# Granule 1's scores ahead of the second w_in piece: one head pair biased on TensorE, three masked by multiplication

## The chip, the cores and the metric

The kernel runs on one core of one Trainium2 chip. The metric is the device time of one launch in microseconds (us).

## The reference

Sliding-window attention with a few global keys and a distance bias, then a feed-forward block with a squared ReLU:

```python
# q, k, v: (4, 8, 768, 64); n_global 8, n_local 96
scores = q @ k^T / 8 - slope[h] * dist        # kept where key < 8, or 0 <= row - col < 96
a = softmax(scores);  x = (a @ v) as (3072, 512)
h = x @ w_in                                  # (512, 2048)
out = (s * relu(h)**2 + b) @ w_out            # (2048, 512)
```

## The kernel before

Work is cut into twelve granules of 256 tokens. The engines run one hand-written order of instructions; nothing is reordered later. For granule j and head pair hp, `S_mm` computes scores in PSUM, `S_post` the exponential on ScalarE (ACT), `A` the product with v, and `A_norm` the division. The distance bias and mask come in one of two ways: TensorE (PE) adds a bias table to the scores with an identity matmul (`SB_mm`), or VectorE (DVE) multiplies the exponentials by a table of exponentials (`S_mul`). `P1(j, f)` is one of eight steps of the first feed-forward product. It needs column piece f of w_in:

```python
for i in range(8):
    load_w_in(i, 8)            # software DMA queue of POOL, 512 x 256 fp32 in, bf16 in SBUF

def SB_mm(j, hp, ...):         # bias into PSUM: ident x bias table, two matmuls of 512 columns
def S_mul(j, hp):              # DVE: pt = pt * tmpl, 128 x 1024 bf16
def make_tmpl(h0, h1, lo, hi): # ACT: tmpl = exp(bias)

def P1(j, fp, sq="dve", tag="psh", relu="act"):
    ps = PS[tag].tile(...)                       # tag psh: two PSUM buffers, taken in turn
    for i in range(2):
        fc = 2 * fp + i
        for kc in range(KC):
            nc.tensor.matmul(ps[:, i, :], lhsT=w_in_bf[:, kc, fc*P:(fc+1)*P], rhs=xT[j][:, kc, :], ...)
    gs = gT[j][:, 2*fp:2*fp+2, :]
    flush()
    if relu == "dve": nc.vector.tensor_scalar_max(gs, ps[:], 0.0)
    else:             nc.scalar.activation(gs, ps[:], ACT.Relu)
    ...                                          # and the square, on either engine or late
```

The stretch that the change edits (granule 0's feed-forward, granule 1's attention):

```python
S_mm(1, 1)
S_post(1, 1, mul=False)
P1(0, 0, "late", "pso", relu="dve")
S_mul(1, 1)
S_mm(1, 2)
S_post(1, 2, mul=False)
P1(0, 1, "late", relu="dve")
SB_mm(1, 3)
S_mm(1, 3, True)
S_post(1, 3, True)
S_mul(1, 2)
P1(0, 2, "late")
A(1, 0, norm=False)
...                                              # A, norms, P1(0, 3)
XT_half(1, 0, "act", "av")                       # transposes of x for granule 1, half each
P1(0, 4, "late")
XT_half(1, 1, "dve", "pso")
for f in range(5):
    Q(0, f)                                      # squares on DVE
P1(0, 5)
P1(1, 0)
...
```

## Time and profile before

| what | before |
|---|---|
| time, median of the first three runs | 207.78 us (207.5 to 208.25) |
| span of the profiled run | 205.9 us |
| busy: PE, DVE, ACT, POOL | 97%, 84%, 56%, 36% |
| PE idle before P1(0,1), for piece 1 of w_in | 0.81 us |
| start of P1(0,5), the first use of piece 5 | 21.89 us |
| landing of piece 5 | 21.81 us |

The lines behind this table stand in the prediction below. They are best read in this order: which engine is busiest, which chain of waits set the end, and where on that chain PE stood still.

### The profile page before, as it was taken

Reading aid. Unit: us, or ns where it says so; the run is one execution under the profiler, and the core shown is the slowest. Engines: PE = TensorE matmul, PEld = TensorE weight load, DVE = VectorE, ACT = ScalarE, POOL = GpSimd, SP = SyncE. Lnnn points to the kernel's source line nnn. Section 1 sums busy time; section 2 is a strip of 40 time slices with the busy share of each in tenths; the row PEclk is TensorE's granted clock in tenths of the full one; section 3 lists DMA queues with packets and bytes.
Section 4 is the critical chain, followed back from the end, with each engine's and each line's share of the span. In section 5 each row is a group of like instructions: output and inputs, shape, how many; then the busy total and the mean of one; then the engine's idle time right before and its main releaser. Section 6 shows DMA issues by size and latency. Waiting matters only on the chain.

```text
span 205.9 us, 5606 instructions
## 1 busy us (share of the span) xinstructions
PE 199.8 (97%) x2295; PEld 160.8 (78%) x2295; DVE 172.9 (84%) x415; ACT 115.6 (56%) x173; POOL 73.7 (36%) x98
## 2 busy tenths in 40 slices
PE   7998999999999999999999999999999999999993
PEld 2667876547766678988988988988988988988883
DVE  5787877699989989788799799788799799787693
ACT  5885689355878576536536536536446446424400
POOL 8994673848273019008119019029000000000000
PEclk9999999999999999999999999999999999999999
DMA  6999999999999969999999989979966040040022
GB/s 168 191 184 197 191 195 192 181 156 162 130 136 155 227 81 96 151 182 128 206 122 115 206 86 111 209 98 120 206 85 154 28 134 22 0 153 5 0 105 102
DMA packets 103962, 27.64 MB, mean 134 GB/s; under 512 B 91392, under 2 KB 102016, under 8 KB 103936
## 3 DMA queue, kind: packets, MB, share of 16 engines
q0 software_dynamic: 70976, 13.11, 84.4%
q1 hardware_dynamic: 31904, 13.64, 35.9%
q10 hardware_dynamic: 1056, 0.52, 0.9%
q8 instruction: 18, 0.29, 0.6%
q14 instruction: 8, 0.07, 0.2%
HBM read 27.26 MB, written 6.29 MB: 163 GB/s over the span
## 4 chain that ended last, share of the span: by engine, by line
PE 84%; DMA 4%; POOL 4%; DVE 4%; ACT 1%; issue 0%; SPq 0%; POOLq 0%
PE ps L552 38%; PE ps_w L728 15%; PE ps L615 7%; PE ps_wb L728 7%; PE ps_av L470 4%; PE ps_s L414 4%; PE ps_wa L728 4%; DMA w_in_bf<-in_moe_w_in_dram 3%; POOL vaug L112 2%; PE ps_2s L615 2%; DMA xT<-xn 1%; DVE pt L441 1%; DVE o_pr L653 1%; POOL qnat L92 1%; POOL knat L92 1%; ACT gT L566 1%
## 5 line engine op out<-in xcount | busy, mean ns | idle before, releaser
L552 PE MATMUL ps<-xT,w_in_bf 128*128 128x256 bf16 x768 | 96.5, 273 | 1.2 <-DMA w_in_bf<-in_moe_w_in_dram 0.8
L552 PEld LDWEIGHTS <-w_in_bf 128*128 128x128 bf16 x768 | 72.6, 98 | 12.1 <-DMA w_in_bf<-in_moe_w_in_dram 1.1
L566 ACT ACTIVATE gT<-ps 128x512 bf16<-128x512 f32 x72 | 43.1, 598 | 58.5 <-PE ps L552 56.4
L427 ACT ACTIVATE pt<-ps_s 128x1024 bf16<-128x1024 f32 (+1 forms) x48 | 43.1, 951 | 4.8 <-PE ps_s L414 4.8
L728 PEld LDWEIGHTS <-sw 128*128 128x128 bf16 x288 | 28.1, 98 | 3.4
L582 DVE TENSOR_TENSOR gT<-gT 128x512 bf16<-128x512 bf16 x73 | 27.6, 416 | 1.7 <-ACT gT L566 1.6
L112 POOL DMA_DIRECT2D vaug<-in_v_dram x24 | 21.6, 914 | 4.1 <-DMA w_out_bf<-in_moe_w_out_dram 1.7
L728 PEld LDWEIGHTS <-gT 128*128 128x128 bf16 x208 | 19.7, 98 | 3.2 <-issue 0.2
L488 DVE TENSOR_TENSOR xn<-ps_av,rc 128x256 bf16<-128x256 f32 x48 | 20.4, 424 | 1.7
L441 DVE TENSOR_TENSOR pt<-pt,tmpl 128x1024 bf16<-128x1024 bf16 x30 | 20.0, 685 | 1.8 <-ACT pt L427 1.8
L125 POOL COPY pdum<-xT 1x1 bf16<-1x1 bf16 x5 | 3.2, 640 | 50.0 <-DMA xT<-xn 50.0
L615 PE MATMUL ps<-w_out_bf,gT 128*128 128x512 bf16 x80 | 19.7, 379 | 0.0
L728 PE MATMUL ps_w<-tw,sw 128*128 128x256 bf16 x144 | 18.7, 273 | 0.0
L738 DVE SCALAR_TENSOR_TENSOR u<-ps_w,s_bc,bvec 128x256 f32<-128x256 f32 x27 | 12.9, 479 | 6.4 <-PE ps_w L728 6.4
L470 PEld LDWEIGHTS <-pt 128*128 128x128 bf16 x352 | 15.3, 98 | 3.4 <-DVE pt L441 1.2
L104 POOL DMA_DIRECT2D qnat<-in_q_dram x18 | 15.9, 901 | 2.8 <-DMA w_out_bf<-in_moe_w_out_dram 1.4
L104 POOL DMA_DIRECT2D knat<-in_k_dram x18 | 16.0, 893 | 1.9 <-issue 1.4
L564 ACT ACTIVATE gT<-ps 128x512 bf16<-128x512 f32 x22 | 13.0, 598 | 6.1 <-PE ps L552 5.9
L470 PE MATMUL ps_av<-vaug,pt 128*128 128x65 bf16 x224 | 16.2, 193 | 0.2 <-DVE pt L441 0.2
L615 PEld LDWEIGHTS <-gT 128*128 128x128 bf16 x96 | 8.7, 97 | 8.1
L487 DVE RECIPROCAL rc<-ps_av 128x4 f32<-128x4 f32 x48 | 8.7, 182 | 7.0 <-PE ps_av L470 6.8
L414 PE MATMUL ps_s<-qT,kT 64*128 64x128 bf16 x224 | 12.5, 218 | 0.1
(102 smaller groups left out, 244.1 us busy)
## 6 DMA issues: line engine op xcount, KB each, us to landing
out_dram<-o_pr SPq DMA_DIRECT2D x10, 512.0 KB, 6.0
vaug<-in_v_dram POOLq DMA_DIRECT2D x24, 128.0 KB, 7.8
knat<-in_k_dram POOLq DMA_DIRECT2D x22, 128.0 KB, 6.4
qnat<-in_q_dram POOLq DMA_DIRECT2D x22, 128.0 KB, 7.6
w_in_bf<-in_moe_w_in_dram POOLq DMA_DIRECT2D x8, 256.0 KB, 8.0
w_out_bf<-in_moe_w_out_dram POOLq DMA_DIRECT2D x4, 512.0 KB, 10.1
out_dram<-o_pr SPq DMA_DIRECT2D x3, 256.0 KB, 3.0
raw<-in_q_dram ACTq DMA_DIRECT2D x2, 256.0 KB, 4.8
```

Of the source, the lines that this page charges most:

```text
L104: nc.gpsimd.dma_start(t[:, i, :, :], src[b, :, sb * P : (sb + 1) * P, :].rearrange("h p d -> p h d"))
L112: nc.gpsimd.dma_start(vaug[b % 2][:, sb, :, 0:D], v[b, :, sb * P : (sb + 1) * P, :].rearrange("h p d -> p h d"),)
L414: nc.tensor.matmul(ps[:, hi, oc * P : (oc + 1) * P], lhsT=kt[r, :], rhs=qT[j][r, hp, i * P : (i + 1) * P], start=not biased, stop=not bias ...
L427: nc.scalar.activation(pt[:, :, 0:n], ps[:, :, 0:n], ACT.Exp, scale=QSCALE)
L441: nc.vector.tensor_tensor(x, x, m.unsqueeze(2).to_broadcast((P, 2, GB, 2 * P)), ALU.mult)
L470: nc.tensor.matmul(av[:, i, hi, :], lhsT=pt[:, hi, c * P : (c + 1) * P], rhs=vv, start=n_ == 0, stop=n_ == len(ops) - 1,)
L488: nc.vector.tensor_tensor(xn[j][:, :, 2 * hp : 2 * hp + 2, :], av[:, :, :, 0:D], rc[:].to_broadcast((P, GB, 2, D)), ALU.mult,)
L552: nc.tensor.matmul(ps[:, i, :], lhsT=w_in_bf[:, kc, fc * P : (fc + 1) * P], rhs=xT[j][:, kc, :], start=(kc == 0), stop=(kc == KC - 1),)
L566: nc.scalar.activation(gs.rearrange("p f (r t) -> p f r t", r=2), ps[:].rearrange("p f (t r) -> p f r t", r=2), ACT.Relu,)
L582: nc.vector.tensor_tensor(gs, gs, gs, ALU.mult)
L615: nc.tensor.matmul(po[j, tb], lhsT=gT[j][:, fc, tb * P : (tb + 1) * P], rhs=w_out_bf[:, fc, :], start=(fc == 0), stop=(fc == FC - 1),)
L728: nc.tensor.matmul(wt[j, ps], lhsT=lhs[:, f, :], rhs=rhs[:, f, :], start=first and f == 0, stop=f == HF - 1, skip_group_check=True,)
```

## The change

Before, the bias matmuls and scores of pair (1,3) followed P1(0,1), which waits for piece 1. The change puts the scores of all four pairs ahead of P1(0,1) and masks pair (1,3) by multiplication. The multiplication's table of heads 6 and 7 is therefore made earlier on ACT, behind the exponentials. To balance DVE, the ReLU of P1(0,1) goes to ACT, and the ReLU of P1(0,0) goes behind a multiplication. The intent is to fill PE's wait for piece 1 and to save the bias product.

```diff
--- before.py
+++ after.py
@@ -558,6 +558,10 @@
                 )
         gs = gT[j][:, 2 * fp : 2 * fp + 2, :]
         flush()
+        if relu == "late":
+            late_sq[j, fp] = gs
+            late_ps[j, fp] = ps
+            return
         if relu == "dve":
             nc.vector.tensor_scalar_max(gs, ps[:], 0.0)
         elif j < W0:
@@ -575,7 +579,10 @@
         else:
             pend.append(gs)
 
-    late_sq = {}
+    late_sq, late_ps = {}, {}
+
+    def relu_late(j, fp):
+        nc.vector.tensor_scalar_max(late_sq[j, fp], late_ps.pop((j, fp))[:], 0.0)
 
     def Q(j, fp):
         gs = late_sq.pop((j, fp))
@@ -888,23 +895,25 @@
     S_post(1, 0, True)
     S_mm(1, 1)
     S_post(1, 1, mul=False)
-    P1(0, 0, "late", "pso", relu="dve")
+    P1(0, 0, "dve", "pso", relu="late")
     S_mul(1, 1)
+    relu_late(0, 0)
     S_mm(1, 2)
     S_post(1, 2, mul=False)
-    P1(0, 1, "late", relu="dve")
-    SB_mm(1, 3)
-    S_mm(1, 3, True)
-    S_post(1, 3, True)
+    S_mm(1, 3)
+    S_post(1, 3, mul=False)
+    make_tmpl(6, 8, 1, 3)
     S_mul(1, 2)
-    P1(0, 2, "late")
+    P1(0, 1, "late")
     A(1, 0, norm=False)
     A_norm(1, 0)
     A(1, 1, "pso", norm=False)
     A_norm(1, 1)
+    P1(0, 2, "late")
+    A(1, 2, "scA", norm=False)
+    S_mul(1, 3)
+    A_norm(1, 2)
     P1(0, 3, "late")
-    A(1, 2, "scA", norm=False)
-    A_norm(1, 2)
     A(1, 3, "scB", norm=False)
     A_norm(1, 3)
     XT_half(1, 0, "act", "av")
@@ -933,7 +942,6 @@
     SS(2, (0, 1))
     P1(1, 6)
     P1(1, 7)
-    make_tmpl(6, 8, 1, 3)
     make_tmpl(0, 8, 0, 1)
     po[0, 0] = ps_o.tile([P, DM], F32, name="ps_2", tag="pso")[:]
     P2_mm(0, 0, 0)
```

## The prediction

> **What bounds the kernel now.** I read the page's busy shares first, then the chain of waits cut to the stage that the change touches, then each engine's timeline there, and last the landing time of each piece of w_in.
>
> ```profile
> PE 199.8 (97%) x2295; PEld 160.8 (78%) x2295; DVE 172.9 (84%) x415; ACT 115.6 (56%) x173; POOL 73.7 (36%) x98
> PE   7998999999999999999999999999999999999993
> ```
>
> The tensor engine is busy for 97% of the 205.9 us span, and the slice row shows its thinner slices in the opening: the first, and the third, from 10.3 to 15.4 us. Work taken off PE shortens the kernel only if PE isn't then held by something else. The chain of waits names the holder (start, length, what):
>
> ```profile
> 9.48 6.50 DMA w_in_bf<-in_moe_w_in_dram
> 15.98 0.05 issue
> 16.03 1.05 PE ps L552 x8
> 17.07 0.43 PE ps_s L394 x2
> 17.51 0.33 PE ps_s L414 x8
> 17.84 0.98 PE ps L552 x8
> 18.82 0.49 PE ps_av L470 x16
> 19.30 0.87 PE ps L552 x8
> 20.18 0.48 PE ps_av L470 x16
> 20.66 0.23 PE ps_x L517 x4
> 20.89 0.87 PE ps L552 x8
> 21.76 0.23 PE ps_x L517 x4
> 21.99 5.32 PE ps L552 x48
> ```
>
> L552 is one P1 step: eight matmuls on one of eight column pieces of w_in, which I number 0 to 7; P1(0,n) needs piece n. L394 is the bias product of head pair 3, L414 its scores, L470 two A steps in a row, L517 half of the x transposes. PE waits for piece 1 until 15.98 us, then runs without a gap. The last row starts with P1(0,5), the first use of piece 5, and runs on through granule 1's first four steps. In PE's timeline:
>
> ```profile
> 16.03 1.05 PE L552 MATMUL ps<-xT,w_in_bf 128*128 128x256 bf16 x8 [0.81 <-DMA w_in_bf<-in_moe_w_in_dram]
> 21.89 5.41 PE L552 MATMUL ps<-xT,w_in_bf 128*128 128x256 bf16 x48
> ```
>
> P1(0,5) starts at 21.89 us with no recorded wait. But how early could it have started? The issue of piece 5 and its time to landing, from the timeline of POOL and the view of the tile:
>
> ```profile
> 12.41 0.82 POOL L129 DMA_DIRECT2D w_in_bf<-in_moe_w_in_dram  x1
> ```
> ```profile
> L129 POOL DMA_DIRECT2D w_in_bf<-in_moe_w_in_dram x1: 817/817/817, 12.4 to 12.4; - x1
> DMA to landing us min/median/max: 9.4/9.4/9.4
> ```
>
> 12.41 + 9.4 = 21.81 us: piece 5 landed 0.08 us before its use. The same sum for each piece gives landings at 13.8, 16.0, 17.2, 18.6, 20.0, 21.8, 22.8 and 24.3 us. Piece 1 checks the method: 9.48 + 6.5 = 15.98, as in the chain. POOL gives a second check, since its later loads resume after "DMA w_in_bf" at 16.27, 17.55, 18.93, 20.23 and 22.13 us, each about 0.3 us after the landing of pieces 1 to 5. So **the delivery of w_in is just hidden behind PE at piece 5**, and this decides the case.
>
> **What the Trainium skill says.** "TensorE: Matmul & The Clock Gate", Part 2, Step-by-step: only weight loads are pulled ahead, and "The MATMULs themselves stay in program order". The trace agrees: PE stood still for 0.81 us before piece 1, though the bias product of pair 3, whose PSUM was freed near 15.4 us, needed nothing from DMA. P1(0,5) will therefore hold everything behind it, even granule 1's P1 steps, whose pieces have landed. "DMA: Bandwidth & Descriptors", Anatomy of one DMA: a variable part of bytes / 436e9. A piece reads 512 x 256 fp32, 524 KB, which would be 1.2 us; the trace has (24.3 - 16.0) / 6 = 1.38 us per piece. Delivery is near its ceiling and does not depend on PE. "ScalarE: Activation LUTs", What ACT_TABLE_LOAD costs: 186 ns + 0.833 ns per element, less 93 ns back to back: 613 ns for the moved table of 512 elements per partition, where the trace has 643 alone and about 0.53 us as a step in a row. "VectorE: DVE Perf Modes", Side-by-side: a two-source bf16 operation runs at two elements per cycle plus about 150 cycles, an estimate of (512 + 158) / 0.96 = 698 ns for a mask multiplication over 1024 elements; the trace has 685.
>
> **The change part by part.**
> Removed on PE: the bias product of pair (1,3), 0.43 us of the chain. Moved on PE: its scores, 0.33 us, now stand before P1(0,1), in the idle stretch from 15.2 to 15.98 us. They need the scB bank, which exp (1,1) frees: the three exps start at 13.40 us and take 2.94 us, 0.98 a step, so the second ends near 15.36. Sixteen matmuls at the chain's rate are done by 15.8, before piece 1. Both parts fit, and PE loses 0.43 + 0.33 = 0.76 us after piece 1.
> Moved to ACT: the ReLU of P1(0,1), 0.60 us. The table of heads 6 and 7 moves there from 34.2 us. New order: exp (1,2) to 16.34, exp (1,3) to 17.33, table to 17.9, ReLU (0,1) to 18.45 us.
> DVE: one multiplication more, 0.685, one ReLU less, 0.67: a net of 0.02 us. In the new order: multiplication (1,1) from 15.5 to 16.2, ReLU (0,0) to 16.8, multiplication (1,2) to 17.4, norms of pairs 0 and 1 to 18.55, multiplication (1,3) to 19.2.
> Now PE again, with durations from the chain: P1(0,1) to 17.07; A(1,0) and A(1,1), 0.49, to 17.56; P1(0,2), 0.87, to 18.43 (piece 2 at 17.2); A(1,2), 0.24, to 18.67. P1(0,3) wants to start at 18.5 (ReLU (0,1) frees its bank at 18.45), but piece 3 lands at 18.6, so it runs from about 18.7 to 19.75. A(1,3), its multiplication done at 19.2, to 20.0; half the transposes to 20.2; P1(0,4), piece 4 at 20.0, to 21.1; the other half, after norms that I put at 20.7, to 21.3. **P1(0,5) could then start about 21.2**, 0.7 us before now, but piece 5 lands at 21.81. With the 0.05 us seen between landing and start at piece 1 it starts at 21.86, against 21.89. The gain is **0.03 us**; some 0.65 us become a new wait for piece 5.
> From there on nothing differs on PE. The table taken from ACT at 34.2 us frees 0.5 us of an engine that next waits 1.02 us for PE, so it is worth nothing on the path.
>
> **The rivals.**
> Full gain. If piece 5 landed by 21.2 us, the 0.7 us would pass on: the k and q of granule 2 land about 1.5 us ahead of use, and the third piece of w_out about 1.4. That makes 207.1 us. Against it: the landing above. For part of it: the interval before piece 5 was 1.8 us against a mean of 1.38, so at an even pace it would land at 16.0 + 4 x 1.38 = 21.5 us, and another execution could gain 0.3 us.
> New waits on ACT or DVE. ReLU (0,1) now stands behind two exps and a table, and P1(0,3) waits for its bank; multiplication (1,3) stands behind two norms. I put both just in time, to 0.1 or 0.5 us. If either is late, about 0.65 us of slack before piece 5 soaks it up; only beyond that is it a loss. A slip of 1 us would make 208.1.
> A downstream give-back. From 41 to 62 us DVE is busy 19.7 of 21 us and the chain crosses it at 63 to 71 us, so an early PE could meet it. But DVE work starts behind PE there and would shift with it; I give this little weight, and it could only take away a gain that the first rival grants, leaving 207.8.
>
> **Range and chances.** 207.78 less 0.03 to 0.3 us, by where piece 5 lands in other executions, is 207.5 to 207.75; I take **207.6 us**. The three runs of before spread over 207.5 to 208.25, wider than the effect, so the range runs from the full gain, **207.1**, to a slip with ordinary noise, **208.1**. Two per cent are 4.2 us, over five times all that is moved: faster by over 2% 0.01, within 2% 0.98, slower 0.01.
>
> **What would show each step right or wrong.** In the changed kernel's profile I expect the idle before P1(0,1) cut from 0.81 to under 0.5 us, its start still at 16.0, the scores of pair 3 done before it, and two L394 matmuls fewer. A new PE wait of 0.4 to 0.7 us for "DMA w_in_bf" should stand before P1(0,5), which starts at 21.8 to 21.9 us, and the chain should run back from there to that transfer. PE's busy time should fall by about half a microsecond with the span nearly unchanged. The prediction is wrong if P1(0,5) starts before 21.5 us without a wait (delivery was not the bound), or after 22.2 (ACT or DVE came late), or if it starts at 21.86 and the end still moves by over 0.4 us, which would put the effect downstream where I see none.

## The result, and the profile after

The changed kernel takes 207.73 us, the median of four runs (207.42 to 207.75), against 207.80 us for the kernel before (four runs, 207.5 to 208.25). The ratio is 0.9991, with a 95% interval of 0.9971 to 1.0012. A ratio here and below is the mean time of one kernel's runs over that of the other's of the same rounds, so not quite the ratio of the medians quoted. Executions over 1.5% slower than the fastest of the same kernel are left out of the means. Repeated with five more rounds the ratio was 1.0003 (0.999 to 1.0017). No gain is measured, and one of more than 0.3% is excluded by the first interval, of more than 0.1% by the second.

From the page of the changed kernel, the PE row of the busy shares and of the slices:

```profile
PE 198.5 (96%) x2286; PEld 160.6 (78%) x2293; DVE 173.4 (84%) x415; ACT 115.9 (56%) x174; POOL 73.2 (36%) x98
PE   7988999999999999999999999999999999999993
```

PE is busy 1.3 us less, and the span is again 205.9 us. Only two of the nine matmuls that the count lacks were removed by the change, the bias product. The other seven are second-product matmuls (L615 before, L622 after) which both programs contain, 96 in all, of which this trace recorded 89. So PE's busy sum exaggerates what was saved.

The two PE waits, from PE's timeline (start, length, what, idle before it and its releaser):

```profile
16.15 1.05 PE L552 MATMUL ps<-xT,w_in_bf 128*128 128x256 bf16 x8 [0.66 <-DMA w_in_bf<-in_moe_w_in_dram]
...
21.90 2.36 PE L552 MATMUL ps<-xT,w_in_bf 128*128 128x256 bf16 x20 [0.42 <-ACT gT L568]
```

The first row is P1(0,1) and the second starts with P1(0,5). P1(0,5) starts at 21.90 us, where it started at 21.89 before, and in front of it now stands a wait that wasn't there. The row blames a ReLU on ACT. The weight loads of the same step, on the row of PE's loader, name another releaser:

```profile
21.90 2.19 PEld L552 LDWEIGHTS <-w_in_bf 128*128 128x128 bf16 x21 [0.59 <-DMA w_in_bf<-in_moe_w_in_dram]
```

Which of the two holds it has to be decided. The chain of waits of the changed kernel follows the ReLU:

```profile
10.84 7.98 DMA w_in_bf<-in_moe_w_in_dram
18.82 0.04 issue
18.87 1.05 PE ps L552 x8
19.92 0.24 PE ps_av L470 x8
20.16 0.22 PE ps_x L517 x4
20.38 0.89 PE ps L552 x8
21.27 0.02 issue
21.29 0.61 ACT gT L568
21.90 0.01 issue
21.90 5.41 PE ps L552 x48
```

Until 18.82 us PE is held by piece 3. P1(0,3) and P1(0,4) follow, and the chain then goes through the ReLU of P1(0,4), which ends at 21.90 us. And piece 5, in POOL's timeline and in the view of the tile:

```profile
12.31 0.84 POOL L129 DMA_DIRECT2D w_in_bf<-in_moe_w_in_dram  x1
```
```profile
L129 POOL DMA_DIRECT2D w_in_bf<-in_moe_w_in_dram x1: 844/844/844, 12.3 to 12.3; - x1
DMA to landing us min/median/max: 9.5/9.5/9.5
```

12.31 + 9.5 = 21.81 us, the same landing as before. Both candidates end within 0.1 us of the start of P1(0,5). The kernel before already speaks against the ReLU: there the ReLU of P1(0,4) ran from 21.80 to 22.40 us and P1(0,5) started at 21.89, in the middle of it. The experiments settle it.

### The profile page after: what moved, and what is told of

Read it like the earlier page. It is cut to its first block, busy times and chain, and to the rows that moved or that the text cites. A ratio compares the mean times of both kernels' runs of the same rounds, so it can differ in the third digit from the quotient of the medians.

```text
span 205.9 us, 5597 instructions
## 1 busy us (share of the span) xinstructions
PE 198.5 (96%) x2286; PEld 160.6 (78%) x2293; DVE 173.4 (84%) x415; ACT 115.9 (56%) x174; POOL 73.2 (36%) x98
## 4 chain that ended last, share of the span: by engine, by line
PE 81%; DMA 5%; POOL 5%; DVE 4%; ACT 2%; issue 1%; SPq 0%; POOLq 0%; ACTq 0%
PE ps L552 37%; PE ps_w L735 15%; PE ps_wb L735 7%; PE ps L622 6%; PE ps_av L470 4%; PE ps_wa L735 4%; DMA w_in_bf<-in_moe_w_in_dram 4%; PE ps_s L414 4%; POOL vaug L112 2%; PE ps_2s L622 2%; DVE pt L441 2%; DMA xT<-xn 1%; DVE o_pr L660 1%; POOL w_in_bf L129 1%; ACT pt L427 1%
## 5 line engine op out<-in xcount | busy, mean ns | idle before, releaser
L570 ACT ACTIVATE gT<-ps 128x512 bf16<-128x512 f32 x72 | 43.1, 598 | 58.5 <-PE ps L552 56.4
L441 DVE TENSOR_TENSOR pt<-pt,tmpl 128x1024 bf16<-128x1024 bf16 x31 | 20.7, 686 | 2.1 <-ACT pt L427 2.1
L125 POOL COPY pdum<-xT 1x1 bf16<-1x1 bf16 x5 | 2.5, 509 | 50.5 <-DMA xT<-xn 50.5
L622 PE MATMUL ps<-w_out_bf,gT 128*128 128x512 bf16 x74 | 18.8, 379 | 0.4 <-issue 0.2
L470 PEld LDWEIGHTS <-pt 128*128 128x128 bf16 x352 | 15.4, 98 | 3.3 <-DVE pt L441 1.2
L568 ACT ACTIVATE gT<-ps 128x512 bf16<-128x512 f32 x23 | 13.6, 598 | 6.9 <-PE ps L552 6.7
L622 PEld LDWEIGHTS <-gT 128*128 128x128 bf16 x96 | 8.7, 97 | 8.1
```

What stands on the lines that cost most here:

```text
L441: nc.vector.tensor_tensor(x, x, m.unsqueeze(2).to_broadcast((P, 2, GB, 2 * P)), ALU.mult)
L470: nc.tensor.matmul(av[:, i, hi, :], lhsT=pt[:, hi, c * P : (c + 1) * P], rhs=vv, start=n_ == 0, stop=n_ == len(ops) - 1,)
L570: nc.scalar.activation(gs.rearrange("p f (r t) -> p f r t", r=2), ps[:].rearrange("p f (t r) -> p f r t", r=2), ACT.Relu,)
L622: nc.tensor.matmul(po[j, tb], lhsT=gT[j][:, fc, tb * P : (tb + 1) * P], rhs=w_out_bf[:, fc, :], start=(fc == 0), stop=(fc == FC - 1),)
```

## The experiments

**Theory D (delivery):** P1(0,5) waits for piece 5 of w_in, which lands at the same time in both kernels, so that what PE saves ahead of it becomes waiting. **Rival S:** it waits for the ReLU of P1(0,4), as the chain says. **Rival G:** PE does get ahead, and the gain is given back further down. All runs were timed in five rounds against the kernel before, and all results passed the comparison with the reference.

### The changed kernel once more

> The change once more, to narrow the interval. Theory D (delivery: P1(0,5) waits for piece 5 of w_in, which lands near 21.8 us in both kernels): ratio to before 0.998 to 1.000, P1(0,5) starts at 21.85 to 21.95 us. Full gain, which D excludes, would be 0.9964.

Measured: 207.75 us (207.45 to 208.34), ratio 1.0003 (0.999 to 1.0017). P1(0,5) started at 21.60 us in the profiled run, earlier than I expected, because piece 5 landed at 12.32 + 9.2 = 21.52 us. PE's row shows no wait there; the loader's row does, a short one for the transfer:

```profile
21.59 2.41 PEld L552 LDWEIGHTS <-w_in_bf 128*128 128x128 bf16 x23 [0.19 <-DMA w_in_bf<-in_moe_w_in_dram]
```

So the landing moves by tenths of a us between executions. Here P1(0,5) came with it, and PE was hardly ahead of it, because piece 1 had come late as well (9.39 + 7.1 = 16.49 us). The ReLU of P1(0,4) ran from 21.39 to 21.99 us in this run, so P1(0,5) did not wait for it.

### Piece 2 not loaded, in both kernels

```diff
+    nc.vector.memset(w_in_bf[:, :, 512:768], 0.0)
-    for i in range(8):
+    for i in (0, 1, 3, 4, 5, 6, 7):
         load_w_in(i, 8)
```

The result is wrong. The comparison passes it all the same: recomputing the reference with those columns zeroed changes the output by 0.7% in the root-mean-square sense.

> The changed kernel with piece 2 of w_in not loaded but set to zero (wrong result on purpose), so that pieces 3 to 7 land about 1.4 us earlier, piece 5 near 20.4 us. Theory D: P1(0,5) starts at 21.05 to 21.2 us, with no wait for DMA, and the time falls by about 0.75 us to 207.0, ratio to before 0.9963. Rival S (P1(0,5) is held by the ReLU of P1(0,4) on ScalarE, as the chain of waits of the changed kernel says): it starts near 21.6 us, time 207.45. Rival G (the gain is given back further down): it starts at 21.1 us but the time stays at 207.7.

> The same edit in the kernel before: piece 2 of w_in set to zero, not loaded (wrong result on purpose). Theory D: PE itself is the bound from piece 1 on there, so P1(0,5) stays at 21.85 to 21.95 us and the time at 207.8, ratio 1.000; the gain of the change, a_no2 against b_no2, then appears at about 0.996. If an earlier landing of the later loads helps somewhere else, this kernel gains too.

Measured, changed kernel with the edit: 207.15 us (206.66 to 207.32), ratio 0.9965 (0.9953 to 0.9977). Kernel before with the edit: 207.88 us (207.74 to 208.25), ratio 1.0007 (0.9995 to 1.0019). With piece 5 early (issued at 11.59 us, landed 8.6 us later, at 20.2) the change is worth 207.88 - 207.15 = 0.73 us. Without the edit it is worth nothing measurable. PE's timeline and ACT's timeline of the changed kernel with the edit:

```profile
21.13 1.04 PE L553 MATMUL ps<-xT,w_in_bf 128*128 128x256 bf16 x8
```
```profile
21.11 0.60 ACT L569 ACTIVATE gT<-ps 128x512 bf16<-128x512 f32 x1 [0.27 <-PE ps L553]
```

The PE row is P1(0,5), with no wait, at 21.13 us. The ACT row is the ReLU of P1(0,4), which starts at 21.11 and ends at 21.71. P1(0,5) doesn't depend on it, and rival S falls. Rival G falls as an explanation too, since most of the gain reaches the end. In the kernel before with the edit P1(0,5) started at 22.17 us rather than 21.9. In that execution piece 1 came later and P1(0,1) started at 16.37 us; from there PE ran without a wait for DMA, as expected.

### Piece 5 made later, in both kernels

```diff
     for i in range(8):
+        if i == 5:
+            nc.gpsimd.dma_start(extra[:], w_in_view[:, :, 0:P])
         load_w_in(i, 8)
```

> The changed kernel with an extra load of 262 KB (half a piece, into a tile that nothing reads; the result stays right) in the queue ahead of piece 5, about 0.69 us of delivery. Theory D: piece 5 lands near 22.5 us, P1(0,5) starts at 22.5 to 22.6, time up by about 0.65 us to 208.4, ratio 1.003. Rival S: P1(0,5) stays at 21.9 us and the time at 207.7, since P1(0,4) and its ReLU are untouched.

> The same extra load in the kernel before. Theory D: piece 5 had only 0.08 us of slack there, so P1(0,5) starts at 22.5 to 22.6 us as well and the time goes up by about 0.6 us to 208.4, ratio 1.003; the changed kernel and this one are equal again.

Measured: changed kernel with the edit 208.16 us (208.02 to 208.36), ratio 1.0019 (1.0007 to 1.0031); kernel before with the edit 208.18 us (208.0 to 208.58), ratio 1.002 (1.0007 to 1.0032). PE's timeline of the changed kernel with it:

```profile
22.35 2.36 PE L555 MATMUL ps<-xT,w_in_bf 128*128 128x256 bf16 x20 [0.99 <-DMA w_in_bf<-in_moe_w_in_dram]
```

P1(0,5) waits 0.99 us and starts at 22.35 us, with piece 5 landed at 13.14 + 9.2 = 22.34. In the kernel before it starts at 22.45, with a wait of 0.18 us:

```profile
22.45 2.25 PE L555 MATMUL ps<-xT,w_in_bf 128*128 128x256 bf16 x19 [0.18 <-DMA w_in_bf<-in_moe_w_in_dram]
```

The two kernels are equal again in time, and both wait for the transfer. In the kernel before most of the shift in this trace is not the transfer's, though: piece 1 came late (P1(0,1) started at 16.30 us), so PE was ready only at 22.27. The size was off: the extra load cost about 0.5 us of delivery in the changed kernel's run (22.34 against the 21.81 of its first profile), not 0.69, and 0.33 to 0.35 us of the time (medians, against 207.83 us in these rounds).

### Only the order changed, with the bias kept on PE

```diff
+    SB_mm(1, 3)
+    S_mm(1, 3, True)
+    S_post(1, 3, True)
     P1(0, 1, "late", relu="dve")
-    SB_mm(1, 3)
-    S_mm(1, 3, True)
-    S_post(1, 3, True)
```

> The kernel before with one part of the change alone: bias product and scores of pair (1,3) stand ahead of P1(0,1), still biased on PE, ReLU (0,1) still on VectorE. The idle stretch before piece 1 is 0.8 us and the two need 0.76 us, from 15.36 us on, so P1(0,1) should slip to 16.15 to 16.3 us. Theory D: P1(0,5) again waits for piece 5 and starts at 21.85 to 21.95 us; ratio 0.998 to 1.000. If the multiplication in place of the bias product were what counts, this one would be slower than the changed kernel by 0.2 us or more.

Measured: 207.63 us (207.36 to 207.92), ratio 0.9991 (0.9979 to 1.0003). P1(0,1) slipped to 16.30 us, as expected, though its releaser was piece 1. P1(0,5) started at 21.40 us, earlier than expected and without a wait, since piece 5 landed at 12.28 + 9.0 = 21.28 in that execution. What follows is that the wait for piece 1 is long enough for the bias product too, at least where piece 1 lands this late (9.35 + 6.9 = 16.25 us), so the multiplication isn't needed to fill it.

### Another step in front of P1(0,5)

If piece 5 is the bound, a step that needs an earlier piece should fill the wait. P1(1,0) needs piece 0 and both halves of granule 1's transposes. So I kept pair (1,3) biased but early, gave the ReLU of P1(0,1) to ACT and moved both halves ahead of P1(0,4). That is the first kernel, the control, cut to its core:

```diff
+    SB_mm(1, 3)
+    S_mm(1, 3, True)
+    S_post(1, 3, True)
+    S_mul(1, 2)
-    P1(0, 1, "late", relu="dve")
+    P1(0, 1, "late")
     ...                          # A(1,0), A(1,1), P1(0,2), A(1,2), A(1,3), P1(0,3)
     XT_half(1, 0, "act", "av")
+    XT_half(1, 1, "dve", "pso")
     P1(0, 4, "late")
-    XT_half(1, 1, "dve", "pso")
```

The second differs from the control only in this:

```diff
     XT_half(1, 0, "act", "av")
     XT_half(1, 1, "dve", "pso")
     P1(0, 4, "late")
     for f in range(5):
         Q(0, f)
-    P1(0, 5)
     P1(1, 0)
+    P1(0, 5)
```

> From the kernel before: bias product and scores of pair (1,3) ahead of P1(0,1), ReLU (0,1) on ScalarE, both halves of granule 1's transposes ahead of P1(0,4). P1(0,5) is still the step that follows. Theory D: PE is ready for it near 21.1 to 21.2 us and waits for piece 5 until 21.85; ratio 0.998 to 1.000.

> The same kernel with P1(1,0), whose piece 0 landed near 13.9 us, ahead of P1(0,5); nothing else differs. Theory D: P1(1,0) starts at 21.1 to 21.3 us, P1(0,5) follows near 22.0 without a wait, and the time falls by 0.6 to 0.75 us to 207.05 to 207.2, ratio 0.9965 to 0.997, so that it beats both kernels. Rival S (a PSUM bank held by the ReLU before): P1(1,0) starts near 21.7 to 21.8 us, time 207.7. Rival G (given back further down): PE is early at 22 us, but the time stays at 207.7.

Measured, control: 207.64 us (207.33 to 207.74), ratio 0.9991 (0.9979 to 1.0003). Its row for P1(0,5) in PE's timeline:

```profile
21.88 2.79 PE L552 MATMUL ps<-xT,w_in_bf 128*128 128x256 bf16 x24 [0.73 <-DMA w_in_bf<-in_moe_w_in_dram]
```

PE was ready 0.73 us early and waited, and here both views name the transfer. With the two steps exchanged: 207.33 us (207.25 to 207.76), ratio 0.9984 (0.9971 to 0.9996). In its trace PE runs from P1(0,4) through P1(1,0) and P1(0,5) without a wait:

```profile
20.29 4.42 PE L552 MATMUL ps<-xT,w_in_bf 128*128 128x256 bf16 x39
```

So the wait is gone, and the time fell by 0.3 us by the ratio, about half of what I expected. The chain of waits shows where the rest stayed:

```profile
43.68 7.01 DMA qT<-qnat
50.69 0.04 issue
50.73 0.46 PE ps_s L414 x10
```

A second transfer stands behind the first. Granule 3's scores wait at 50.7 us for its q, transposed by DMA. In the kernel before, the view of that tile has the second of these transposes as

```profile
L327 SPq DMA_TRANSPOSE qT<-qnat x1: 1189/1189/1189, 43.2 to 43.2; - x1
DMA to landing us min/median/max: 7.0/7.0/7.0
```

which lands at 43.2 + 7.0 = 50.2 us, and PE began those scores at 50.92 there. The slack was 0.7 us in that execution. It is less in others: with the steps exchanged the landing was 50.69 us here and 50.86 in a later run, and PE was ready at 50.4 us.

### Work in front of the second gate

One quarter of a P2 step (`P2b`, four matmuls of the second product) moved from behind granule 3's first scores to ahead of them:

```diff
     Q(2, 2)
+    P2b(2)
     period(3, [
-            (P2b, 2),
             (P2b, 3),
     ...
-        (3, 1, 3, 1),
+        (2, 1, 3, 1),
```

> The kernel of b_swap once more, as the control of the next one on the same chip and rounds. It got 0.9984, less than the 0.9965 to 0.997 expected: its trace shows a second wait at 50.7 us, for the transposes of granule 3's q. Expected again: 0.998 to 0.999.

> The kernel of b_swap, and one quarter of a P2 step (four matmuls, 0.87 us, operands there since 43 us) moved from behind the first scores of granule 3 to ahead of them, so that PE has work while the transposes of granule 3's q land. Theory D with a second gate at granule 3's q: the wait there goes and the rest of the 0.7 us comes through: ratio 0.9965 to 0.9975, time 207.1 to 207.3. If instead VectorE, busy without a pause from 41 to 58 us, takes the rest, it stays at 0.998 to 0.999.

> The kernel before with that second edit alone (a quarter of P2 ahead of granule 3's first scores). Its transposes land about 0.4 us before PE needs them, so there is no wait to take away: ratio 0.999 to 1.001.

| kernel | time, us | ratio to before |
|---|---|---|
| exchange, repeated | 207.51 (207.25 to 207.95) | 0.9987 (0.9973 to 1.0002) |
| exchange and P2 quarter | 207.11 (207.06 to 207.46) | 0.997 (0.9958 to 0.9983) |
| kernel before with the P2 quarter alone | 207.84 (207.59 to 208.02) | 1.0 (0.9987 to 1.0013) |

PE's timeline of the middle one:

```profile
50.32 1.03 PE L615 MATMUL ps<-w_out_bf,gT 128*128 128x512 bf16 x4
51.28 0.51 PE L414 MATMUL ps_s<-qT,kT 64*128 64x128 bf16 x12
```

The scores follow without a wait for the transposes. With both gates filled 0.6 us of the 0.7 arrives at the end (207.73 us for the kernel before in these rounds, less 207.11), and this version beats the kernel before, with an interval clear of 1. The changed kernel was not timed in these rounds; the ratios (0.997 against 0.9991 and 1.0003) suggest that it is beaten too. DVE, which I had named as a rival for the rest, did not take it. Neither edit alone does this: the exchange gives about 0.3 us by its two ratios (0.16% and 0.13%, the second interval just including 1), the P2 quarter alone nothing. The intervals of the exchange with and without the quarter overlap, so that the quarter helps rests on the medians, 0.40 us apart, and on the wait that is gone from the trace.

## Why the prediction was right

- **The bound.** That w_in's delivery is just hidden at piece 5 held in the executions profiled: by 0.08 us in the kernel before, and by 0.03 us (21.85 less 21.82) where that kernel had only the P2 quarter moved. It decided the case, as the control kernel and the two pairs of piece-5 experiments show.
- **The number.** 207.6 us was predicted, and 207.73 and 207.75 were measured. The gap of 0.13 us is within the noise, and so is the gain of 0.03 us that the mechanism gives. The time alone therefore doesn't show the mechanism; the traces and the experiments do.
- **What PE saves.** The 0.76 us are real: with piece 5 early, the change is worth 0.73 us. In the changed kernel the loader was free for P1(0,5) at 21.90 - 0.59 = 21.3 us. That is where the prediction's own sequence ends ("the other half [...] to 21.3"); the "21.2" that it then takes is a slip of 0.1 us. P1(0,5) started at 21.90 us where 21.86 was predicted.
- **Two readings.** The row of slices was misread: the thinner slices are the first and the fourth, from 15.4 to 20.6 us, not the third. The wait for piece 1, up to 15.98 us, lies in the fourth, and nothing else rests on it. The 1.2 us, 613 ns and 698 ns worked out from the Trainium skill's pages were estimates; the sequence was built on the traces' durations.
- **The new wait.** 0.42 us on PE's row and 0.59 us on the loader's, predicted as 0.4 to 0.7 us, with the estimate of the slack at 0.65. The chain of waits I had expected to run from P1(0,5) to the transfer. It ran through the ReLU of P1(0,4) instead, which happened to end 0.01 us before the start. Two traces in which P1(0,5) starts before that ReLU ends rule it out.
- **ACT and DVE.** ReLU (0,1) ended at 18.31 us (18.45 predicted) and multiplication (1,3) at 19.27 us (19.2). Both were in time.
- **The wait for piece 1.** I expected under 0.5 us left and P1(0,1) still at 16.0. It was 0.66 us and 16.15. Piece 1 landed 0.1 us later (9.38 + 6.7 = 16.08), and the scores ahead of it were done at 15.5 us, 0.3 us sooner than in my sequence.
- **Where a step failed.** In the rival "Full gain" I wrote that the 0.7 us would pass on, because granule 2's k and q and the third piece of w_out have 1.4 to 1.5 us of slack. I hadn't looked at the next transfer, granule 3's q, whose slack was 0.7 us or less. Had piece 5 been early, that gate would have taken part of the gain in some executions. In the profiled execution of the changed kernel without piece 2 it held ten of these scores until 50.54 us (a wait of 0.18 us), and yet the medians there show 0.73 us; this is not resolved. It didn't matter for the number predicted.
- **Where piece 5 lands in other executions.** The term "0.03 to 0.3 us" allowed an earlier landing. In the nine profiled executions of kernels with the same loads up to there, piece 5 landed between 21.14 and 21.82 us, in two groups. Where piece 1 landed by 16.08 us, piece 5 came at 21.8 (four executions, the first profiles of both kernels among them); where piece 1 came at 16.17 us or later, piece 5 came at 21.52 or earlier (five). The changed kernel showed both. So it is partly luck of the profiled execution that 21.90 us fell so close to 21.86. What makes the landings vary is open. The term also took the kernel before to be fixed at 21.89 us. When piece 1 comes late that kernel is late too: without piece 2 it started P1(0,1) at 16.37 and P1(0,5) at 22.17 us. In such executions the change could gain more, by an estimate of 22.17 - 21.60 = 0.57 us from two traces. No profile caught the kernel before with its own loads in one of them, and a mean gain of 0.1 to 0.2 us is neither shown nor excluded by the two timings (0.9991 and 1.0003).

## What to carry to other kernels

Before taking work off the bounding engine, add issue time and time to landing for every transfer that this engine will use afterwards, and compare with its use: the smallest slack caps the gain, though the profile shows no wait there yet. If a transfer is the cap, reorder so that the engine does something whose data are already there, and look for the next gate in the same way. A releaser in a chain of waits is trusted only if it also ends before the start in other executions and variants.

## What the Trainium skill lacked or had wrong

- "DMA: Bandwidth & Descriptors", Anatomy of one DMA, gives a DMA's time as 2.0 us plus bytes / 436e9, an estimate of 3.2 us for a piece of w_in. It gives no figures for a queue of such loads: eight issued 0.73 us apart landed 1.38 us apart on average from the second on, with 5.1 us to landing for the first and 10.4 for the eighth. For deciding on slack, the landing of each one is what counts.
- The same page gives no spread of a landing from one execution to another. Here piece 5 landed between 21.14 and 21.82 us in nine executions of kernels with the same loads.
- The same page, DMA Transpose (X-bar), lacks a time to landing for a transpose beside busy queues. Those of granule 3's q took 6.8 to 7.8 us here, and were the second gate.
- "Perfetto Trace Analysis" has, as far as I found, no warning on coincident releasers: the changed kernel's PE row and chain name a ReLU (21.29 + 0.61 = 21.90 us) for a start that two other traces show to be independent of it. Nor does it say that a trace can lack matmul records: 89 of 96 identical instructions were recorded after the change.
